# Attention, FFN and gate for one token: wide FFN reads, and the first and last DMA outside the block

## Chip, cores and metric

The kernel runs on one core of one Trainium2 chip. The metric is the device time of one execution in microseconds (us), of which the median of several runs is given. Engines are named as in the profile: PE does matmuls (PEld is its weight load), DVE is the vector engine, ACT the scalar engine, POOL GpSimd, SP the sync engine, which here only issues DMAs. A core has 16 DMA engines that all queues share.

## Reference

Four sequences (B = 4) decode one token each. Attention reads the last 4,096 positions of a cache with 8 key/value heads that 32 query heads share; beside it runs a gated FFN on the same `x`; a sigmoid gate mixes the two.

```python
x = A_x                                                   # 4 x 1 x 512, bf16
g = sigmoid((x * gate_w).sum(-1, keepdims=True))
# A: attention
q = (x @ wq) as 32 heads of 128
k, v = last 4096 positions of k_cache, v_cache            # 4 x 8 x 16384 x 128
p = softmax(q . k * 128 ** -0.5)
a = (p . v) as 4096 columns @ wo                          # wo: 4096 x 512
# B: FFN
gate = x @ W_gate;  up = x @ W_up                         # 512 x 1792 each
h = gate * (gate > 0) * up
b = h @ W_down                                            # 1792 x 512
return g * a + (1 - g) * b                                # 4 x 1 x 512
```

## The kernel before

The work on the caches is cut into NSET = 8 sets: set `s` is half of the key/value heads (four) of sequence `s // 2`. A set's keys are one load of 4 MB into `Ksb[:, s % 2]`, its values one of 4 MB into `Vsb[:, s % 2]`; each of the 128 partitions gets 32,768 contiguous bytes. So two sets of keys and two of values can be in SBUF or on their way, and a load waits until the set that used its buffer two before is done: the keys' load on the last scores (`SC`, s - 2), the values' load on the last `PV` of s - 2.

For each set, PE transposes the keys in place (L340, 16 groups of four, evicted by ACT at L345 or DVE at L347), computes scores (L373), DVE masks them and takes the maximum (L381, L388 to L402), ACT takes the exponent (L410), DVE transposes the probabilities (L417), PE multiplies with the values (L429), and `combine` sums the pieces and writes the set's normalised rows into `oq` (L450). The PE instructions of sets 2 to 7 run in a loop of three turns.

All large loads go through SP's DMA queue, in program order: `wq` (4 MB into `Wbig`, L245), K0, then K and V in turn, then behind V6 the two FFN matrices `W_gate` (L250) and `W_up` (L252), 1,792 KB each, into the free `Ksb[:, 0]`, then V7, then `W_down` (L255) into the free `Vsb[:, 0]`, then `wo` in four pieces (L260; 2,048, 1,280, 512 and 256 KB) into `Wbig`, where `wq` was. An FFN matrix of 1.8 MB lies in 128 partitions of 14,336 contiguous bytes: `(p t) f -> p (t f)` gives partition `p` four rows of `W_gate`, and `(p i) w -> p (i w)` fourteen rows of `W_down`. ACT's queue has two small loads, `x` (L243) and `gate_w` (L244).

At the end PE computes gate and up (`gateup`, L477), DVE makes `hT` (L481 to L483), PE does the last set's values and its `combine`, then `W_down` (L545) and `wo` (L553) into one PSUM bank `AB`. There the 512 output columns are cut into four blocks of 128: block `cb` accumulates in partitions 32 cb and on. `oq` and `hT` give each matmul 32 weight columns, of which columns 0, 8, 16 and 24 hold the four sequences and the rest are zero. So block `cb` of sequence `b` stands in row 32 cb + 8 b of `AB`. One DVE copy (L557) takes the bank to `outs`, 128 x 128, and the store (L558) reads every eighth row of it: 16 pieces of 256 bytes.

The program is first listed and then written out engine by engine (`Program`). An operation names the event that it gives and those that it waits for; `plan` works out the semaphore counts and leaves out waits already made; `put` writes the waits and the instruction; `emit` writes an engine's whole list. SP's list begins with the load of `wq` and ends with a bare wait for the store (L559). All five lists are written inside `nc.Block()` (L562): each engine branches into its part, and at the block's end all engines meet in a barrier, which the profile shows under L562. Ahead of the block stands another barrier, under L595, behind the setting of a few constants.

Of the kernel before, what the change touches and what calls it, by code (L numbers as in the profile page):

```python
# [6 lines left out]
BF16 = mybir.dt.bfloat16  # L7
ACTF = mybir.ActivationFunctionType
# [10 lines left out]
FF = 1792  # L19
NSET = 8  # L20
NFT = FF // 128
# [12 lines left out]
class Program:  # L34
# [69 lines left out]
            if name is not None:  # L104
                ins.then_inc(sems[self.events[name][0]], step)

    def emit(self, engine, eng, sems):
        ops, plan = self.ops[engine], self.plan(engine)
        if engine != "pe":
            for op, need in zip(ops, plan):  # L110
                self.put(eng, sems, op, need)
            return
        n = len(self.turns) - 1
        base = []
        for t in range(n + 1):
            level = {}
            for need in plan[:self.turns[t]]:
                level.update({s: v for s, v in need.items() if s in self.lowered})
            base.append(level)
        shift = [{s: base[t + 1].get(s, 0) - base[t].get(s, 0) for s in self.lowered} for t in range(n)]  # L120
        length = self.turns[1] - self.turns[0]
        bodies = []
        for t in range(n):
            assert shift[t] == shift[0] and self.turns[t + 1] - self.turns[t] == length
            body = []
            for k in range(length):
                need = plan[self.turns[t] + k]
                body.append({s: v - base[t].get(s, 0) for s, v in need.items() if s in self.lowered})
                if t > 0:
                    assert all(s in self.lowered for s in need), (t, k, need)  # L130
                    a, b = ops[self.turns[t] + k][1], ops[self.turns[0] + k][1]
                    assert (a is None) == (b is None) and (a is None or self.events[a][0] == self.events[b][0])
            bodies.append(body)
            assert body == bodies[0], [(k, x, y) for k, (x, y) in enumerate(zip(body, bodies[0])) if x != y]
        for k in range(self.turns[0]):
            self.put(eng, sems, ops[k], plan[k])
        for s, v in base[0].items():
            eng.sem_inc(sems[s], -v)
        with eng.Fori(0, n):
            for k in range(length):  # L140
                i = self.turns[0] + k
                need = dict(bodies[0][k])
                need.update({s: v for s, v in plan[i].items() if s not in self.lowered})
                self.put(eng, sems, ops[i], need)
            for s, v in shift[0].items():
                if v:
                    eng.sem_inc(sems[s], -v)
        for i in range(self.turns[n], len(ops)):
            self.put(eng, sems, ops[i], {s: v - base[n].get(s, 0) if s in self.lowered else v
                                         for s, v in plan[i].items()})  # L150


def bass_gated_mix__sliding_block_cached__glu_gated_reglu__decode_kernel(
# [13 lines left out]
    with ExitStack() as ctx:  # L167
        def sb(name, shape, dt):
            return ctx.enter_context(nc.sbuf_tensor(name, shape, dt))

        Ksb = sb("Ksb", [128, 2, 16384], BF16)
        Vsb = sb("Vsb", [128, 2, 16384], BF16)
# [30 lines left out]
        recip = sb("recip", [128, 2], FP32)  # L203
        oq = sb("oq", [128, 32, 32], BF16)
        gtmp = sb("gtmp", [128, NFT * 4], FP32)
        gtmp2 = sb("gtmp2", [128, NFT * 4], FP32)
        hT = sb("hT", [128, NFT, 32], BF16)
        outs = sb("outs", [128, 128], BF16)
        banks = [ctx.enter_context(nc.psum_tensor("bank%d" % i, [128, 512], FP32)) for i in range(8)]
        TR = banks[0:NTR]  # L210
        SCB = banks[NTR:NTR + NSC]
# [27 lines left out]
        def load_v(s):  # L239
            P.dma("sp", lambda e: e.dma_start(Vsb[:, s % 2, :], heads(A_v_cache, s)), ("V", s),  # L240
                  [("PV", s - 2, 3)] if s >= 2 else [], slot="v%d" % (s % 2))

        P.dma("act", lambda e: e.dma_start(xsb[0:4, :], A_x.rearrange("b o d -> (b o) d")), ("X",))  # L243
        P.dma("act", lambda e: e.dma_start(xsb[4:5, :], gate_w.rearrange("(o d) -> o d", o=1)), ("GW",))  # L244
        P.dma("sp", lambda e: e.dma_start(Wbig[:, :], A_wq.rearrange("(p t) w -> p (t w)", p=128)), ("WQ",))  # L245
        load_k(0)
        for s in range(1, NSET):
            load_k(s)
            load_v(s - 1)
        P.dma("sp", lambda e: e.dma_start(Ksb[:, 0, 0:4 * FF], B_W_gate.rearrange("(p t) f -> p (t f)", p=128)),  # L250
              ("WG",), [("SC", NSET - 2, NBANK - 1)])
        P.dma("sp", lambda e: e.dma_start(Ksb[:, 0, 4 * FF:8 * FF], B_W_up.rearrange("(p t) f -> p (t f)", p=128)),  # L252
              ("WU",), [("SC", NSET - 2, NBANK - 1)])
        load_v(NSET - 1)
        P.dma("sp", lambda e: e.dma_start(Vsb[:, 0, 0:NFT * 512], B_W_down.rearrange("(p i) w -> p (i w)", p=128)),  # L255
              ("WD",), [("PV", NSET - 2, 3)])
        wo_src = A_wo.rearrange("(p i) w -> p (i w)", p=128)
        for k in range(len(WO_CUTS) - 1):
# [178 lines left out]
        def combine(s):  # L437
            par, b, half = s % 2, s // 2, s % 2
            r = slice(64 * half, 64 * half + 64)
            for k in range(8):  # L440
                lo = 3 - k % 4 + 64 * (k // 4)
                P.op("pe", lambda e, k=k, lo=lo: e.matmul(FB[r, 256:288], Wsel[:, lo:lo + 64], osb[:, par, 32 * k:32 * k + 32],  # L442
                                                          start=(k == 0), stop=(k == 7)), None,
                     [("OSB", s), ("WSUM",), ("QC", 1), ("G",), ("OQ", s - 1) if s >= 1 else None, ("H",) if s == NSET - 1 else None])
            P.op("pe", lambda e: e.matmul(FB[r, 288:288 + NPIECE], Wsum[:, :], rowsum[:, par, :], start=True, stop=True),
                 ("SUMS", s))
            P.op("dve", lambda e: e.tensor_reduce(ssum[r, par:par + 1], FB[r, 288:288 + NPIECE], AXIS.X, ALU.add),
                 ("SSUM", s), [("SUMS", s)])
            P.op("dve", lambda e: e.reciprocal(recip[r, par:par + 1], ssum[r, par:par + 1]), ("RECIP", s), [("SSUM", s)])
            P.op("dve", lambda e: e.tensor_scalar(oq[r, :, 8 * b], FB[r, 256:288], recip[r, par:par + 1],  # L450
                                                  gsb[r, b:b + 1], op0=ALU.mult, op1=ALU.mult),
                 ("OQ", s), [("RECIP", s), ("G",), ("OQZ",)])

# [18 lines left out]
        def gateup():  # L472
            for i in range(NFT):
                for which, W, key in ((0, Wg, "WG"), (1, Wu, "WU")):
                    col = 64 + 64 * which + 4 * i
                    for t in range(4):
                        P.op("pe", lambda e, W=W, i=i, t=t, col=col: e.matmul(  # L477
                            FB[:, col:col + 4], W[:, t, i:i + NFT * 127 + 1:NFT], xT[:, t * 8:t * 8 + 4],
                            start=(t == 0), stop=(t == 3)),
                            ("GU",) if (i == NFT - 1 and which == 1 and t == 3) else None, [("WG",), ("WU",), ("OQ", NSET - 2)])  # L480
            P.op("dve", lambda e: e.tensor_scalar(gtmp[:, :], FB[:, 64:64 + NFT * 4], 0.0, None, op0=ALU.max), ("H0",), [("GU",)])  # L481
            P.op("dve", lambda e: e.tensor_tensor(gtmp2[:, :], FB[:, 128:128 + NFT * 4], gtmp[:, :], ALU.mult), ("H1",), [("H0",)])
            P.op("dve", lambda e: e.tensor_tensor(  # L483
                hT[:, :, :].rearrange("p i (b o) -> p i b o", o=8)[:, :, :, 0], gtmp2[:, :].rearrange("p (i b) -> p i b", b=4),
                gsb[:, 4:8].rearrange("p (o b) -> p o b", o=1).to_broadcast([128, NFT, 4]), ALU.mult), ("H",),
                [("H1",), ("G",), ("HZ",)])

# [61 lines left out]
        for k in range(len(WO_CUTS) - 1):  # L549
            for i in range(WO_CUTS[k], WO_CUTS[k + 1]):  # L550
                for cb in range(4):
# [2 lines left out]
                        AB[32 * cb:32 * cb + 32, 0:128], oq[:, i, :], Wo3[:, i, cb * 128:(cb + 1) * 128],  # L554
                        start=False, stop=(i == 31), tile_position=(0, 32 * cb)),
                        ("ACC",) if last else None, [("WO", k), ("OQ", NSET - 1)])
        P.op("dve", lambda e: e.tensor_copy(outs[:, :], AB[:, 0:128]), ("OUTS",), [("ACC",)])  # L557
        P.dma("sp", lambda e: e.dma_start(out.rearrange("b o (c d) -> c (b o) d", d=128), outs[0:128:8, :]), ("OUT",), [("OUTS",)])  # L558
        P.op("sp", None, None, [("OUT",)])  # L559

        sems = {name: ctx.enter_context(nc.semaphore(name)) for name in P.sems}
        with nc.Block() as block:  # L562
            @block.sync
            def _(e):
                P.emit("sp", e, sems)

            @block.gpsimd
            def _(e):
                P.emit("pool", e, sems)

            @block.tensor
            def _(e):
                P.emit("pe", e, sems)

            @block.vector
            def _(e):
                P.emit("dve", e, sems)

            @block.scalar
            def _(e):  # L580
                P.emit("act", e, sems)


# [26 lines left out]
```

## Time and profile before

| what | value |
|---|---|
| median of 3 runs | 197.55 us (197.55, 197.55, 197.69) |
| the profiled execution, its own time | 197.38 us |
| its span | 195.7 us |
| PE, DVE, ACT busy | 72%, 53%, 47% of the span |
| packets of SP's queue | 3,476, 81.01 MB |
| HBM read over the span | 414 GB/s |
| mean granted PE clock | 0.89 of full speed |
| first DMA of SP issued | 0.81 us |
| last matmul's result copied (L557) | 193.19 us |
| store issued (L558) | 193.51 us |

The span goes from the first to the last instruction that the profile shows; the execution's own time has in addition what lies before and after it. Times in the profile count from the span's start. A busy PE is not a PE at its peak, and idle time of an engine that isn't the bottleneck costs nothing. SP's issue of a DMA is not the transfer: between them stand the queue and what was queued before. The profile also keeps a record of each DMA packet (start, duration, bytes, queue), and among them the 4-byte writes by which each of the 16 engines reports the end of its share of a load; those are called landing records here.

### The profile page before, as it was taken

The numbers are of one execution on the slowest core, as the hardware profiler recorded it, in microseconds if no ns is written. First come the engines' busy times: TensorE is split into PE (matmuls) and PEld (weight loads), VectorE is DVE, ScalarE is ACT, GpSimd is POOL, SyncE is SP. The second block draws the span as 40 slices with busy tenths as digits, with TensorE's granted clock in tenths as the row PEclk, the third lists the DMA queues.
The fourth block names the chain that finished last, engine by engine and source line by source line (L and its number), as shares of the span: only waits on it lengthen the run. The fifth ranks groups of instructions, "written<-read, shape, count | busy, mean of one in ns | idle before, by whom it ended". The sixth has DMA issues, their size and how long they took to land.

```text
span 195.7 us, 4263 instructions
## 1 busy us (share of the span) xinstructions
PE 140.6 (72%) x1858; PEld 107.7 (55%) x1858; DVE 103.6 (53%) x278; ACT 91.5 (47%) x108; POOL 7.9 (4%) x39
## 2 busy tenths in 40 slices
PE   0134199968889919992999399929992999498634
PEld 0034197535567518751976286528752875397533
DVE  2102025888599456945585659456945584741200
ACT  2000058698398409760886098509750976220000
POOL 7400000000000000000000000000000000000000
PEclk9999999999999996997599879996996699965855
DMA  6999999999999999999999999999999999999991
GB/s 215 449 429 452 429 449 442 425 429 437 432 422 429 425 429 429 427 429 425 435 429 435 429 429 430 429 429 429 429 429 429 435 411 425 450 431 415 422 385 59
DMA packets 3498, 81.19 MB, mean 415 GB/s; under 512 B 409, under 2 KB 414, under 8 KB 670
## 3 DMA queue, kind: packets, MB, share of 16 engines
q1 hardware_dynamic: 3476, 81.01, 96.8%
q8 instruction: 9, 0.15, 0.3%
q14 instruction: 3, 0.02, 0.0%
q10 hardware_dynamic: 10, 0.01, 0.0%
HBM read 81.01 MB, written 0.00 MB: 414 GB/s over the span
## 4 chain that ended last, share of the span: by engine, by line
DMA 57%; PE 25%; ACT 9%; DVE 4%; issue 1%; SPq 1%
DMA Ksb<-in_A_k_cache_dram 46%; PE bank L340 16%; DMA Wbig<-in_A_wo_dram 12%; ACT Ksb L345 7%; PE bank L373 5%; DVE Ksb L347 2%; PE bank L429 2%; ACT sc L410 2%; PE bank L553 1%; PE bank L442 1%; DVE pT L417 1%; ACT L410 1%; DVE sc L381 1%; SPq L260 0%; DVE oq L450 0%
## 5 line engine op out<-in xcount | busy, mean ns | idle before, releaser
L345 ACT ACTIVATE Ksb<-bank 128x1024 bf16<-128x1024 bf16 x72 | 70.9, 1022 | 68.2 <-PE bank L340 68.0
L340 PE MATMUL bank<-identf,Ksb 128*128 128x128 f32 x512 | 81.1, 313 | 29.4 <-DMA Ksb<-in_A_k_cache_dram 24.0
L340 PEld LDWEIGHTS bank<-identf,Ksb 128*128 128x128 f32 x512 | 66.6, 161 | 44.1 <-DMA Ksb<-in_A_k_cache_dram 25.7
L347 DVE COPY Ksb<-bank 128x1024 bf16<-128x1024 bf16 x56 | 38.0, 685 | 41.8 <-PE bank L340 40.8
L381 DVE CUSTOM_DVE_ANT_0 sc<-bank,mask 128x512 bf16<-128x512 f32 x32 | 21.7, 684 | 9.6 <-PE bank L373 9.5
L429 PE MATMUL bank<-Vsb,pT 128*32 128x256 bf16 x512 | 20.8, 291 | 0.9 <-DMA Vsb<-in_A_v_cache_dram 0.9
L373 PE MATMUL bank<-Ksb,QSP 128*32 128x512 bf16 x256 | 19.4, 383 | 2.1 <-DVE Ksb L347 1.6
L410 ACT ACTIVATE sc<-sc,negmax 128x1024 bf16<-128x1024 bf16 x16 | 18.3, 1146 | 4.8 <-DVE negmax L402 4.7
L417 DVE STREAM_TRANSPOSE pT<-sc 128x1024 bf16<-128x1024 bf16 x16 | 19.7, 1237 | 1.3 <-ACT sc L410 1.0
L429 PEld LDWEIGHTS bank<-Vsb,pT 128*32 128x32 bf16 x512 | 13.2, 101 | 7.1 <-issue 3.3
L442 PEld LDWEIGHTS bank<-osb,Wsel 128*64 128x64 f32 x128 | 8.1, 138 | 4.6 <-issue 2.6
L442 PE MATMUL bank<-osb,Wsel 128*64 128x32 f32 x128 | 8.9, 224 | 1.2 <-DVE osb L434 1.2
L373 PEld LDWEIGHTS bank<-Ksb,QSP 128*32 128x32 bf16 x256 | 4.1, 94 | 9.4 <-DVE Ksb L347 4.4
L477 PE MATMUL bank<-xT,Ksb 128*128 128x4 bf16 x112 | 6.9, 199 | 1.8 <-DVE oq L450 1.8
L477 PEld LDWEIGHTS bank<-xT,Ksb 128*128 128x128 bf16 x112 | 6.8, 160 | 1.9 <-issue 1.9
L553 PE MATMUL bank<-Wbig,oq 128*32 128x128 bf16 x128 | 4.2, 311 | 4.1 <-DMA Wbig<-in_A_wo_dram 4.0
L357 POOL COPY QSP<-QS 128x64 bf16<-128x64 bf16 x8 | 1.8, 236 | 118.2 <-PE bank L373 107.4
L457 PE MATMUL bank<-xT,Wbig 128*128 128x4 bf16 x128 | 3.6, 166 | 4.0 <-DMA Wbig<-in_A_wq_dram 4.0
L306 PE MATMUL bank<-ident,xsb 5*128 5x5 bf16 x4 | 0.3, 167 | 7.9 <-DMA xsb<-in_gate_w_dram 7.9
L553 PEld LDWEIGHTS bank<-Wbig,oq 128*32 128x32 bf16 x128 | 3.1, 140 | 5.0 <-DMA Wbig<-in_A_wo_dram 5.0
L457 PEld LDWEIGHTS bank<-xT,Wbig 128*128 128x128 bf16 x128 | 3.5, 104 | 4.0 <-DMA Wbig<-in_A_wq_dram 4.0
L434 DVE COPY osb<-bank 128x256 f32<-128x256 f32 x8 | 3.4, 420 | 3.6 <-PE bank L429 3.6
(55 smaller groups left out, 47.0 us busy)
## 6 DMA issues: line engine op xcount, KB each, us to landing
Ksb<-in_A_k_cache_dram SPq DMA_DIRECT2D x8, 4096.0 KB, 22.9
Vsb<-in_A_v_cache_dram SPq DMA_DIRECT2D x8, 4096.0 KB, 32.0
Wbig<-in_A_wq_dram SPq DMA_DIRECT2D x1, 4096.0 KB, 12.2
Wbig<-in_A_wo_dram SPq DMA_DIRECT2D x1, 2048.0 KB, 20.2
Ksb<-in_B_W_gate_dram SPq DMA_DIRECT2D x1, 1792.0 KB, 17.9
Ksb<-in_B_W_up_dram SPq DMA_DIRECT2D x1, 1792.0 KB, 21.8
Vsb<-in_B_W_down_dram SPq DMA_DIRECT2D x1, 1792.0 KB, 15.6
Wbig<-in_A_wo_dram SPq DMA_DIRECT2D x1, 1280.0 KB, 22.8
```

The source lines that it names most:

```text
L340: P.op("pe", lambda e, bk=bk, cc=cc, c=c, s=s: e.transpose(bk[:, cc * 128:(cc + 1) * 128], kw[:, c * 128:(c + 1) * 128], identf[:, :]), (" ...
L345: P.op("act", lambda e: e.activation(dst, bk[:, :].bitcast(BF16), ACTF.Copy), ("KTC", s, i), [("KT", s, i)])
L347: P.op("dve", lambda e: e.tensor_copy(dst, bk[:, :].bitcast(BF16)), ("KTC", s, i), [("KT", s, i)])
L373: P.op("pe", lambda e, a=a, h=h: e.matmul(bk[32 * a:32 * a + 32, 0:512], QSP[:, s % 2, h, :], k4[:, 16 * bank:16 * bank + 16, 32 * a:32 * ...
L381: P.op("dve", lambda e: e.tensor_tensor_reduce(sc[:, s % 2, bank * 512:(bank + 1) * 512], bk[:, :], mask[:, :], 1.0, LOWEST, ALU.add, ALU.max,
L410: P.op("act", lambda e: e.activation(sc[:, par, k * PW:(k + 1) * PW], sc[:, par, k * PW:(k + 1) * PW], ACTF.Exp, bias=negmax[:, par:par + ...
L417: P.op("dve", lambda e: e.transpose(pT[:, par, k * PW:(k + 1) * PW], sc[:, par, k * PW:(k + 1) * PW]), ("PTT", s, k), [("EXP", s, k), ("PV ...
L429: P.op("pe", lambda e, c=c, g=g, col=col: e.matmul(OB[32 * g:32 * g + 32, 0:256], pT[:, par, col:col + 32], v3[:, 16 * k + c, :], start=(k ...
L442: P.op("pe", lambda e, k=k, lo=lo: e.matmul(FB[r, 256:288], Wsel[:, lo:lo + 64], osb[:, par, 32 * k:32 * k + 32], start=(k == 0), stop=(k ...
L457: P.op("pe", lambda e, h=h, t=t: e.matmul(FB[:, 64 + 4 * h:68 + 4 * h], Wq3[:, t, 128 * h:128 * h + 128], xT[:, t * 8:t * 8 + 4], start=(t ...
L477: P.op("pe", lambda e, W=W, i=i, t=t, col=col: e.matmul(FB[:, col:col + 4], W[:, t, i:i + NFT * 127 + 1:NFT], xT[:, t * 8:t * 8 + 4], star ...
L553: P.op("pe", lambda e, i=i, cb=cb: e.matmul(AB[32 * cb:32 * cb + 32, 0:128], oq[:, i, :], Wo3[:, i, cb * 128:(cb + 1) * 128], start=False, ...
```

## The change

1. `emit` takes a range of the engine's list. SP's first operation, the load of `wq`, is written before the block is entered; its last, the bare wait for the store, behind the block's end; all others inside as before.
2. A helper `wide` adds a DMA instruction whose two sides have different shapes. `W_gate`, `W_up` and `W_down` are read as 32 rows of 57,344 bytes; the destination stays 128 partitions of 14,336 bytes. Each row read fills four partitions. Bytes, order in the queue and waits are the same.
3. `oq` and `hT` hold the four sequences in the weight columns 0 to 3 in place of 0, 8, 16 and 24. Block `cb` of sequence `b` then stands in row 32 cb + b of `AB`.
4. `outs` is 4 x 512. Four copies bring the blocks there, 0 and 2 on DVE, 1 and 3 on ACT, and the store is 4 rows of 1,024 bytes, which waits for both engines.

```diff
-    def emit(self, engine, eng, sems):
+    def emit(self, engine, eng, sems, lo=0, hi=None):
         ops, plan = self.ops[engine], self.plan(engine)
         if engine != "pe":
-            for op, need in zip(ops, plan):
+            for op, need in list(zip(ops, plan))[lo:hi]:
                 self.put(eng, sems, op, need)
             return
...
-        outs = sb("outs", [128, 128], BF16)
+        outs = sb("outs", [4, 512], BF16)
...
+        def wide(e, dst, src):
+
+            return e.add_instruction(mybir.InstDMACopy(
+                mode="Copy", name=nc.get_next_instruction_name(), engine=e.engine, queue="qSPDynamicHW",
+                ins=[e.lower_ap_dma(src)[0]], outs=[e.lower_ap_dma(dst)[0]]))
...
-        P.dma("sp", lambda e: e.dma_start(Ksb[:, 0, 0:4 * FF], B_W_gate.rearrange("(p t) f -> p (t f)", p=128)),
+        P.dma("sp", lambda e: wide(e, Ksb[:, 0, 0:4 * FF], B_W_gate.rearrange("(p t) f -> p (t f)", p=32)),
               ("WG",), [("SC", NSET - 2, NBANK - 1)])
-        P.dma("sp", lambda e: e.dma_start(Ksb[:, 0, 4 * FF:8 * FF], B_W_up.rearrange("(p t) f -> p (t f)", p=128)),
+        P.dma("sp", lambda e: wide(e, Ksb[:, 0, 4 * FF:8 * FF], B_W_up.rearrange("(p t) f -> p (t f)", p=32)),
               ("WU",), [("SC", NSET - 2, NBANK - 1)])
         load_v(NSET - 1)
-        P.dma("sp", lambda e: e.dma_start(Vsb[:, 0, 0:NFT * 512], B_W_down.rearrange("(p i) w -> p (i w)", p=128)),
+        P.dma("sp", lambda e: wide(e, Vsb[:, 0, 0:NFT * 512], B_W_down.rearrange("(p i) w -> p (i w)", p=32)),
               ("WD",), [("PV", NSET - 2, 3)])
...
-            P.op("dve", lambda e: e.tensor_scalar(oq[r, :, 8 * b], FB[r, 256:288], recip[r, par:par + 1],
+            P.op("dve", lambda e: e.tensor_scalar(oq[r, :, b], FB[r, 256:288], recip[r, par:par + 1],
...
-                hT[:, :, :].rearrange("p i (b o) -> p i b o", o=8)[:, :, :, 0], gtmp2[:, :].rearrange("p (i b) -> p i b", b=4),
+                hT[:, :, 0:4], gtmp2[:, :].rearrange("p (i b) -> p i b", b=4),
...
-        P.op("dve", lambda e: e.tensor_copy(outs[:, :], AB[:, 0:128]), ("OUTS",), [("ACC",)])
-        P.dma("sp", lambda e: e.dma_start(out.rearrange("b o (c d) -> c (b o) d", d=128), outs[0:128:8, :]), ("OUT",), [("OUTS",)])
+        for c in range(4):
+            to, src = outs[0:4, 128 * c:128 * c + 128], AB[32 * c:32 * c + 4, 0:128]
+            if c % 2 == 0:
+                P.op("dve", lambda e, to=to, src=src: e.tensor_copy(to, src), ("OUTS", c), [("ACC",)])
+            else:
+                P.op("act", lambda e, to=to, src=src: e.activation(to, src, ACTF.Copy), ("OUTS", c), [("ACC",)])
+        P.dma("sp", lambda e: e.dma_start(out.rearrange("b o d -> (b o) d"), outs[:, :]), ("OUT",), [("OUTS", c) for c in range(4)])
         P.op("sp", None, None, [("OUT",)])
...
+        P.emit("sp", nc.sync, sems, 0, 1)
         with nc.Block() as block:
             @block.sync
             def _(e):
-                P.emit("sp", e, sems)
+                P.emit("sp", e, sems, 1, -1)
...
+        P.emit("sp", nc.sync, sems, -1)
```

## Prediction

> **What bounds the kernel now.** I read the views in this order: the page's 40 slices and its DMA queues, the chain of waits from its end backwards, the packet counts of two stretches, and the timeline of the first two and the last four microseconds. The median of the three runs is 197.55 us; the profiled execution took 197.38, of which its span is 195.66 (195.7 on the page) and 1.72 lies around it. The sum below is made against 197.38, and 0.17 is added at the end.
>
> The page, slices and queues (queue: packets, MB, share of 16 engines):
>
> ```profile
> DMA  6999999999999999999999999999999999999991
> ...
> q1 hardware_dynamic: 3476, 81.01, 96.8%
> q8 instruction: 9, 0.15, 0.3%
> ```
>
> Sixteen DMA engines are busy from the first slice to the last: the packet records have no idle moment on any of them between about 4 and 190 us. So what counts is when the slowest engine has moved its share of the 81 MB, and what lies before its first and after its last packet. Compute only waits. The end of the chain (start us, us, what):
>
> ```profile
> 168.06 22.77 DMA Wbig<-in_A_wo_dram
> 190.83 0.04 issue
> 190.87 1.85 PE bank L553 x56
> 192.72 0.01 issue
> 192.74 0.43 PE bank L553 x8
> 193.17 0.02 issue
> 193.19 0.29 DVE outs L557
> ```
>
> The last four loads are the pieces of `wo`, issued near 168 and landed behind everything queued before them. The packet records put the last byte of the last piece at 192.27; PE sees it at 192.73 and needs 0.43 for eight matmuls. PE also waited before pieces 1 and 2 (PEld 1.44 and 0.25 us), so a stream that ends earlier by a fraction of a microsecond takes the end with it.
>
> **The FFN reads.** 3 x 128 packets of 14,336 bytes become 3 x 32 rows of 57,344: each engine reads two rows for a matrix where it read eight, 18 packets fewer in all. The addresses and the partitions they fill are the same. What a packet costs beyond its bytes comes from two stretches of the queue, the first (129 to 157 us) with 32,768-byte packets alone, the second (160 to 166) with 14,336-byte ones:
>
> ```profile
> q1 hardware_dynamic: 411, 12.12, 100.6%
> ```
>
> ```profile
> q1 hardware_dynamic: 196, 2.58, 101.3%
> ```
>
> 12.12 MB are 370 data packets (the rest are 4-byte semaphore writes of 9 ns), so 1.006 x 16 x 28 us, less 0.37, over 370 gives 1.217 us a packet. 2.58 MB are 180 packets, so 1.013 x 16 x 6, less 0.14, over 180 gives 0.5395. The slope is 0.6775 us over 18,432 bytes, 36.76 ns a KB (of 1,000 bytes), and 0.5395 - 0.527 leaves 12.5 ns a packet. The landing records, 9.71 us for eight large packets and 4.30 for eight small ones, leave 10.8. 18 packets fewer are worth 0.19 to 0.23 us: I take **-0.21**. If that fixed part belongs to writing a partition's 14,336 bytes, which are as many as before, nothing is gained: 0 is the upper end inside this theory, and -0.25 the lower (the median packets, 1.214 and 0.539, leave 14 ns each).
>
> The Trainium skill speaks against this edit: DMA: Bandwidth & Descriptors, section Why small descriptors are slow, puts the fixed cost at about 3 cycles a packet and calls joining descriptors worth it only up to 256 bytes. With its 850 MHz, 18 x 3.5 ns would be 0.06, an estimate from that page, and the sum below would be 197.05 in place of 196.90. The trace's 11 to 12.5 ns are over three times as much, and I go by the trace.
>
> Where these loads land is covered: W_gate and W_up are down by 168.41 in the landing records, and PE reaches them at 170.89 behind `oq` of L450; W_down lands at 182.40 and is used from 183.97. If that cover were gone, a late row would stall PE by its lateness, but PE still has 2.87 us of waiting for the first piece of `wo`. SP issues them in 0.33 to 0.43 us, long before their turn.
>
> **The head.** The `wq` load leaves the block, still behind the launch barrier. Timeline of the first two microseconds:
>
> ```profile
> 0.80 0.56 ACTq L243 DMA_DIRECT2D xsb<-in_A_x_dram  x1
> ...
> 0.81 0.39 SPq L245 DMA_DIRECT2D Wbig<-in_A_wq_dram  x1
> ...
> 1.40 0.23 ACTq L244 DMA_DIRECT2D xsb<-in_gate_w_dram  x1
> ```
>
> SP leaves the barrier at 0.74 and issues at 0.81; only that step into the block is passed, no other SP instruction, and no other queue's. The first packet follows the issue by 1.02 us (1.83) and should move with it: **-0.05**, between -0.07 and 0.
>
> **The tail.** One 128x128 copy becomes four of 4x128, two on DVE and two on ACT; the store becomes four rows of 1,024 bytes instead of sixteen of 256; SP goes through the block's closing barrier first and waits for the store after it. What stands there now, timeline, then SP's waits, then the instructions of the block's line:
>
> ```profile
> 193.51 0.69 SPq L558 DMA_DIRECT2D out_dram<-outs  x1
> ```
>
> ```profile
> SPq L562 <- DMA out_dram<-outs: 1.1, 1, 1.1
> ```
>
> ```profile
> L562 SPq COMPARE_BRANCH  x1: 32/32/32, 195.3 to 195.3; - x1
> L562 SPq DRAIN  x1: 13/13/13, 195.4 to 195.4; - x1
> L562 SPq EVENT_SEMAPHORE  x1: 17/17/17, 195.6 to 195.6; - x1
> ```
>
> - Copies. A DVE copy of 128 columns took 0.29. Four small DVE operations on different partition groups are this row:
>
> ```profile
> 169.29 0.67 DVE L402 TENSOR_SCALAR negmax<-mall 32x1 f32<-32x1 f32 x4
> ```
>
> (0.67 - 0.145)/3 is 0.175 from start to start, 0.03 above one's 0.145; so a second copy adds up to 0.32, at least 0.15 if they overlap. ACT's pair is no later: 0.17 for the four columns of L318 and 0.83 ns a further column (1022 ns at 1024) make 0.28 each, and ACT has been idle since 172. **+0.28**.
> - SP now waits for two engines, ACT behind DVE: **+0.03** (0 to 0.06), a semaphore instruction of 17 ns and its neighbour. Behind this wait stands only the store.
> - The store. The old form had its first packet at 194.81, 1.30 after its issue began. The nearest row is the load of `x`, also four rows of 1,024 bytes: packet at 1.76 after an issue at 0.80, 0.96. **-0.34**; gate_w's single row (1.99 after 1.40) would make it -0.71, no change 0. From the last packet (194.93) to SP's release (195.28) stays 0.35.
> - The exit. From 195.28 to 195.66 SP branches, drains and passes the barrier, 0.38. In the new order this runs while the store is in flight (SP is free at about 194.3, the answer is due near 195.2), and 0.02 remains: **-0.36**, at worst 0 if the launch's end takes it back. Its cover is the store's 1.1 us; were that under 0.4, the rest would show again.
>
> Tail: 0.28 + 0.03 - 0.34 - 0.36 = -0.39. The new columns of `oq` and `hT` change strides, not shapes: 0 each, L450's 0.43 us being 3 us ahead of the first piece of `wo`.
>
> **Sum.** -0.21 - 0.05 - 0.39 = -0.65: 197.38 becomes 196.73, and against the median **196.90**.
>
> **Rivals.** *Half of it is empty*: the fixed cost sits on the writing side (0) and the store's latency does not depend on its form (0). Then -0.05 + 0.31 - 0.36 = -0.10, 197.45. For it: the page counts packets, not which side costs; against it: the same four-row form at the head answered in 0.96.
>
> *Long rows are slower.* Place: the three FFN loads. A single read of 57,344 bytes has to feed four partitions, and no row of this trace is longer than 32,768. The slowest packets here, the instruction fetches of 16,384 bytes, took 1.05 us, 15.6 bytes a ns. At that rate six rows an engine cost 22.0 us against 24 x 0.5395 = 12.9: +9.1, less 0.44 for the rest, 206.2. It decides already where a row takes over 2.29 us (25 bytes a ns; four packets now take 2.16), which makes the kernel slower by 0.2%. Against it: longer packets were always a little faster here, and the addresses stay in the same order.
>
> *A fetch strikes a late engine.* The engines end the first piece of `wo` between 185.21 and 187.30, though `wq` landed within 0.54 us on all: the landing records show each instruction fetch setting one engine back by about 1.5 us (at 177.83 one due at 180.51 landed at 182.05), and so far each struck an engine not struck before. Were an order of fetches changed so that one struck one of the last group, the end moves by +1.5: 198.4. For it: DVE, ACT and SP get other instruction counts; against it: PE, which has nearly all instructions, keeps its own.
>
> **How the numbers follow.** The likeliest as worked: 0.62, own range 196.4 to 197.2 (most of the store's bound on one side, of the exit's on the other). Half empty: 0.25. Long rows slow: 0.07. Fetch: 0.06. The range is **196.4 to 197.7**: it takes in the half-empty case and leaves the two slow ones, 0.13, and a little below. A measurement of this kernel tells about 0.2%, 0.4 us, from no change. Faster by more (under 197.15): 0.58 of the first case and 0.05 of the second, **0.63**; within: 0.04 and 0.19, **0.23**; slower: 0.13 and 0.01, **0.14**.
>
> **What would show it.** FFN packets of 57,344 bytes of about 2.11 us and a last `wo` byte near 192.0: right; 2.16, or packets still of 14,336: the first rival; over 2.29: the second. The store's first packet about 0.96 us after its issue, SP's closing barrier ahead of the store's landing, and a span that ends within 0.05 of SP's release. The `wq` issue near 0.76. A spread over 2.1 us between the first and the last engine's landing of `wo` speaks for the third. The prediction is wrong if any transfer starves a stage before 168 us, where I expect nothing to move by more than the head's 0.05.

## The result and the profile after

The changed kernel takes 196.70 us (median of 6 runs, 196.32 to 196.77) against 197.61 for the kernel before (median of 6, 197.50 to 198.00): ratio 0.9949, 95% interval 0.9936 to 0.9962, so 0.75 to 1.26 us less. The forecast was 196.9 in a range of 196.4 to 197.7, faster by 0.65. The profiled execution took 196.66 with a span of 195.33; what lies around the span is 1.33, where it was 1.72.

That last pair of numbers is the first thing to see. Between the two profiled executions the span lost 0.33 us, the remainder 0.39. The page after, slices and queues:

```profile
DMA  6999999999999999999999999999999999999892
...
q1 hardware_dynamic: 3176, 81.01, 97.0%
q8 instruction: 9, 0.15, 0.3%
```

300 packets fewer for the same 81.01 MB: the 384 FFN packets became 96, and 12 of the store's 16 are gone. The DMA engines are as full as before, and there are still nine instruction fetches. The end of the chain of waits (start us, us, what):

```profile
168.76 22.25 DMA Wbig<-in_A_wo_dram
191.05 1.84 PE bank L559 x44
```

The end still hangs on the last pieces of `wo`. In the packet records their last byte lands at 192.45, 0.18 later than before, although every byte is the same: the stream has not become shorter in this pair of executions. What got shorter lies behind it. Timeline of the last microseconds:

```profile
192.91 0.40 PE L559 MATMUL bank<-Wbig,oq 128*32 128x128 bf16 x8
193.37 0.56 ACT L568 ACTIVATE outs<-bank 4x128 bf16<-4x128 f32 x2 [20.60 <-PE bank L559]
193.37 0.59 DVE L566 CAST outs<-bank 4x128 bf16<-4x128 f32 x2 [7.43 <-PE bank L559]
194.03 0.35 SPq L569 DMA_DIRECT2D out_dram<-outs  x1
```

The instructions of the block's closing line (POOL's and SP's), and SP's waits (line; count; ns; first and last start):

```profile
L574 POOLq EVENT_SEMAPHORE  x2: 17/17/17, 194.6 to 194.7; - x2
...
L574 SPq DRAIN  x1: 167/167/167, 194.4 to 194.4; - x1
L574 SPq EVENT_SEMAPHORE  x1: 17/17/17, 194.7 to 194.7; - x1
```

```profile
L101 SPq EVENT_SEMAPHORE  x2: 17/17/17, 194.0 to 195.3; - x2
```

SP is through the barrier at 194.76 (POOL at 194.72), while the store is still on its way (its last packet ends at 194.97); SP's own wait, the second of L101, is released at 195.32 and is the span's last instruction. From the start of the first copy to the end of the span it was 195.66 - 193.19 = 2.47 before and is 195.33 - 193.37 = 1.96 now.

The stretch from 160 to 166 us of the FFN reads (packets, MB, share of 16 engines):

```profile
q1 hardware_dynamic: 57, 2.29, 89.6%
```

40 rows of 57,344 bytes; (0.896 x 16 x 6 - 0.15) / 40 is 2.147 us each. Four packets of before took 4 x 0.5395 = 2.158. Whether the stream gains this difference is asked under "What a packet costs beyond its bytes".

The head, timeline:

```profile
0.80 0.40 SPq L251 DMA_DIRECT2D Wbig<-in_A_wq_dram  x1
```

It is issued at 0.803 where it was 0.811, and the first packet starts at 1.83 as before.

### The profile page after: what moved, and what is told of

Read it like the earlier page. It is cut to its first block, busy times and chain, and to the rows that moved or that the text cites. A ratio compares the mean times of both kernels' runs of the same rounds, so it can differ in the third digit from the quotient of the medians.

```text
span 195.3 us, 4267 instructions
## 1 busy us (share of the span) xinstructions
PE 143.7 (74%) x1858; PEld 109.8 (56%) x1858; DVE 104.0 (53%) x279; ACT 92.2 (47%) x110; POOL 8.0 (4%) x39
## 3 DMA queue, kind: packets, MB, share of 16 engines
q1 hardware_dynamic: 3176, 81.01, 97.0%
HBM read 81.01 MB, written 0.00 MB: 415 GB/s over the span
## 4 chain that ended last, share of the span: by engine, by line
DMA 57%; PE 27%; ACT 8%; DVE 5%; issue 1%; SPq 1%; DVEq 0%
DMA Ksb<-in_A_k_cache_dram 45%; PE bank L346 18%; DMA Wbig<-in_A_wo_dram 11%; ACT Ksb L351 6%; PE bank L379 5%; DVE Ksb L353 3%; PE bank L435 2%; ACT sc L416 1%; PE bank L559 1%; PE bank L448 1%; DVE pT L423 1%; ACT L416 1%; DVE sc L387 1%; SPq L266 0%; SPq L245 0%
## 5 line engine op out<-in xcount | busy, mean ns | idle before, releaser
L346 PE MATMUL bank<-identf,Ksb 128*128 128x128 f32 x512 | 82.4, 316 | 28.2 <-DMA Ksb<-in_A_k_cache_dram 23.0
L448 PEld LDWEIGHTS bank<-osb,Wsel 128*64 128x64 f32 x128 | 8.8, 148 | 4.8 <-issue 2.8
L448 PE MATMUL bank<-osb,Wsel 128*64 128x32 f32 x128 | 9.7, 233 | 1.2 <-DVE osb L440 1.2
L568 ACT ACTIVATE outs<-bank 4x128 bf16<-4x128 f32 x2 | 0.5, 270 | 20.6 <-PE bank L559 20.6
```

Source lines behind the costliest of these rows:

```text
L346: P.op("pe", lambda e, bk=bk, cc=cc, c=c, s=s: e.transpose(bk[:, cc * 128:(cc + 1) * 128], kw[:, c * 128:(c + 1) * 128], identf[:, :]), (" ...
```

## Experiments

The ratio of each run is to the kernel before, measured on the same chip beside it; its median there was 197.61 in the first group, 197.55 in the second, 197.51 in the third. "Remainder" is a run's time less its span, as a median over its runs (spans are given to 0.1 us); for the kernel before it is 1.74 to 1.78.

**The theory after the result (T)**: nearly all of the gain is the place of SP's wait, half of it inside the span and half around it; the store's new form gives a little, long rows and head nothing. Against it: the prediction's own sizes (P), and that the remainder fell because of the store's form (S).

### One part at a time

Long rows alone (`e1_wide_only`):

```diff
-        P.dma("sp", lambda e: e.dma_start(Ksb[:, 0, 0:4 * FF], B_W_gate.rearrange("(p t) f -> p (t f)", p=128)),
+        P.dma("sp", lambda e: wide(e, Ksb[:, 0, 0:4 * FF], B_W_gate.rearrange("(p t) f -> p (t f)", p=32)),
...
```

> The kernel before with the three FFN matrices read in rows of 57,344 bytes and nothing else. Theory T (the gain sits in the place of the wait; a long row costs what its four parts did): FFN packets of 2.14 us, landings of each matrix 4.27 to 4.29 us apart, time lower by 0.00 to 0.06 us, ratio 0.9997 to 1.0. Theory P (the prediction: 12.5 ns less for each packet that falls away): packets of 2.11 us, time lower by 0.21, ratio 0.9989.

Measured: 197.53, ratio 0.9997 (0.9988 to 1.0006), remainder 1.73. Median packet 2.144 us, the landings of each of the two first matrices 4.29 us behind those of the load before it (mean of the 16 engines), as in the kernel before. The interval holds no change, and P's 0.9989 barely; packets and landings decide for T. By the landings nothing of the predicted gain is there.

The wait alone (`e2_exit_only`):

```diff
-                P.emit("sp", e, sems)
+                P.emit("sp", e, sems, 0, -1)
...
+        P.emit("sp", nc.sync, sems, -1)
```

> The kernel before with nothing changed but SP's wait for the store, which stands behind the block. Theory T: 0.36 us less inside the span and 0.39 less around it (1.72 to 1.33), so 0.75 in all, ratio 0.9962. Theory P: 0.36 inside the span and the same 1.72 around it, ratio 0.9982. Theory S (what lies around the span fell because of the store's new form): as P here.

Measured: 196.78, ratio 0.9958 (0.9945 to 0.9972), remainder 1.38. The block's line (POOL and SP) and SP's wait in this kernel:

```profile
L562 POOLq EVENT_SEMAPHORE  x2: 17/17/17, 194.9 to 194.9; - x2
...
L562 SPq DRAIN  x1: 423/423/423, 194.4 to 194.4; - x1
...
L562 SPq EVENT_SEMAPHORE  x1: 17/17/17, 195.0 to 195.0; - x1
```

```profile
L101 SPq EVENT_SEMAPHORE  x1: 17/17/17, 195.4 to 195.4; - x1
```

With the old store form the remainder fell all the same, so S is out, and P's 0.9982 lies outside the interval. This one edit carries 0.83 of the 0.91 us between the medians.

Copies, columns and store alone (`e3_store_only`), the wait inside the block:

```diff
-        P.op("dve", lambda e: e.tensor_copy(outs[:, :], AB[:, 0:128]), ("OUTS",), [("ACC",)])
+        for c in range(4):
+            to, src = outs[0:4, 128 * c:128 * c + 128], AB[32 * c:32 * c + 4, 0:128]
...
```

> The kernel before with columns 0 to 3, the four copies and the store of four rows; the wait stays inside the block. Theory T: from the end of the last matmul to the store's issue +0.33 us, from issue to first packet -0.53, so 0.20 less, ratio 0.9990, and 1.72 around the span. Theory P: +0.31 and -0.34, ratio 0.9998. Theory S: 0.20 less in the span and 0.39 less around it, ratio 0.9970.

Measured: 197.37, ratio 0.9987 (0.9978 to 0.9996), remainder 1.75. Timeline of its end:

```profile
193.45 0.56 ACT L562 ACTIVATE outs<-bank 4x128 bf16<-4x128 f32 x2 [21.55 <-PE bank L553]
193.45 0.59 DVE L560 CAST outs<-bank 4x128 bf16<-4x128 f32 x2 [8.39 <-PE bank L553]
194.10 0.35 SPq L563 DMA_DIRECT2D out_dram<-outs  x1
```

0.65 from copies to issue (0.32 before, so +0.33), and the packet records have the first packet at 194.88, 0.78 after the issue (1.30 before, so -0.52). By the rows that is 0.19 less, as T has it; P's 0.9998 is just outside the interval, and S is out again.

The changed kernel without the head (`e4_no_head`):

```diff
-        P.emit("sp", nc.sync, sems, 0, 1)
...
-                P.emit("sp", e, sems, 1, -1)
+                P.emit("sp", e, sems, 0, -1)
```

> The changed kernel with the load of wq back inside the block, all else as changed. Theory T: SP's first issue 0.01 us later, time as the changed kernel's within 0.05, ratio to the kernel before 0.995. Theory P: 0.05 later, ratio 0.9952.

Measured: 196.63, ratio 0.9947 (0.9933 to 0.9960), remainder 1.29. Inside or outside the block, the load of `wq` is issued at 0.803: the head is worth nothing that can be seen.

### Where the 0.4 us around the span went

Theory E: after the barrier each engine has a way out of the program that the profile does not show. Before, all five began it together at the span's end; now four begin it 0.6 us earlier and only SP's own still follows the store. Rival B: it matters only that no barrier stands behind the store. All five engines wait (`e5_all_wait`):

```diff
-        P.emit("sp", nc.sync, sems, -1)
+        nc.sync.wait_ge(sems["d_OUT"], 16)
+        nc.gpsimd.wait_ge(sems["d_OUT"], 16)
+        nc.tensor.wait_ge(sems["d_OUT"], 16)
+        nc.vector.wait_ge(sems["d_OUT"], 16)
+        nc.scalar.wait_ge(sems["d_OUT"], 16)
```

> The changed kernel, but all five engines wait for the store behind the block, not SP alone. Theory E (the 0.39 us less around the span is the other engines' way out of the program, which runs while SP alone still waits): span as changed, 195.3 to 195.5, but around it 1.7 to 1.8 again, time 0.3 to 0.5 above the changed kernel's 196.7, ratio 0.997. Theory B (it is the barrier that no longer stands behind the store): around it 1.3 as changed, ratio 0.995.

Measured: 197.14, ratio 0.9982 (0.9973 to 0.9990), remainder 1.77, span as in the changed kernel. No barrier stands behind the store here, and yet the remainder is back. B is out.

The same edit with one engine in place of SP:

> The changed kernel, but ACT in place of SP waits for the store behind the block. Theory E: ACT's own way out decides; if all engines' ways are alike, 196.7 as with SP; if they differ, up to 0.4 more or less than that. Theory B: 196.7.

> The changed kernel, but POOL in place of SP waits for the store behind the block. Theory E: 196.7 if the ways out are alike, up to 0.4 more or less if not. Theory B: 196.7.

> The changed kernel, but PE in place of SP waits for the store behind the block. Theory E: 196.7 if the ways out are alike, up to 0.4 more or less if not. Theory B: 196.7.

> The changed kernel, but DVE in place of SP waits for the store behind the block. Theory E' (each engine has its own way out; the span's remainder was 1.31 us with SP waiting, 1.43 with ACT, 1.53 with PE, 1.77 with POOL): a remainder between 1.3 and 1.8, time 196.6 to 197.2. If the remainder is 1.3 or less whichever engine but POOL waits, the table of the others is chance.

| who waits for the store | median us | ratio (interval) | remainder us |
|---|---|---|---|
| in the block, before the barrier | 197.61, 197.55, 197.51 | 1 | 1.74 to 1.78 |
| SP (the changed kernel) | 196.70 | 0.9949 (0.9936 to 0.9962) | 1.31 |
| DVE | 196.64 | 0.9954 (0.9940 to 0.9967) | 1.34 |
| ACT | 196.68 | 0.9959 (0.9946 to 0.9972) | 1.43 |
| PE | 196.88 | 0.9966 (0.9954 to 0.9979) | 1.53 |
| POOL | 197.16 | 0.9984 (0.9975 to 0.9992) | 1.77 |
| all five | 197.14 | 0.9982 (0.9973 to 0.9990) | 1.77 |

The last instruction of the span with POOL waiting, from the line of that wait:

```profile
L595 POOLq EVENT_SEMAPHORE  x1: 17/17/17, 195.2 to 195.2; - x1
```

In that execution the span is 0.16 shorter than the changed kernel's, 195.18, and the run still takes longer: POOL's way out is some 0.45 us longer than SP's and sets the end whenever POOL waits, alone or with the others. (A remainder also holds what lies before the span; only the differences between engines are read here.) That fits E, and it explains the kernel before: there POOL left the barrier within 0.1 us of all the others, and the remainder is POOL's, 1.74 to 1.78. With SP waiting, POOL leaves at 194.72, so 194.72 + 1.77 = 196.49 against SP's 195.33 + 1.31 = 196.64: SP's end is the later one by only 0.15. In the run with the wait alone the barrier is later, and the two are level: POOL 194.96 + 1.77 = 196.73, SP 195.44 + 1.31 = 196.75. The step from SP to DVE and ACT is within the spread of the runs.

What a way out consists of stays open, since the profile does not show it. A closing handshake that passes the engines in a fixed order would give such a table as well as five separate ways of different length, and no run here tells the two apart.

### A store in two halves

If a store's answer goes with its rows, two stores of eight rows on two queues would beat both kernels (`e10_two_stores`; the wait behind the block, one copy, old columns):

```diff
+        for h, q in ((0, "sp"), (1, "act")):
+            P.dma(q, lambda e, h=h: e.dma_start(out.rearrange("b o (c d) -> c (b o) d", d=128)[2 * h:2 * h + 2],
+                                                outs[64 * h:64 * h + 64:8, :]), ("OUT", h), [("OUTS",)])
+        P.op("sp", None, None, [("OUT", 0), ("OUT", 1)])
```

> The kernel before with the wait behind the block, one 128x128 copy, columns 0, 8, 16, 24, and two stores of eight rows of 256 bytes, blocks 0 and 1 by SP, 2 and 3 by ACT; SP waits for both. Against the run with the wait alone behind the block (196.8): if a store's time to its first packet goes with its rows ([4,4] took 1.30 us, [4,1] 0.77), about 1.0 us, and 0.2 to 0.3 less, 196.5, ratio 0.9945, faster than the changed kernel; if it goes with the number of its dimensions, 1.3 as before and 196.8, ratio 0.996.

Measured: 196.96, ratio 0.9970 (0.9958 to 0.9982): a miss. Timeline:

```profile
193.59 0.67 SPq L559 DMA_DIRECT2D out_dram<-outs  x1
193.59 0.64 ACTq L559 DMA_DIRECT2D out_dram<-outs  x1
```

Each half takes nearly as long to issue as the whole did (0.69), and its first packet is 1.27 us behind its issue on SP and 1.53 on ACT. Going from 16 rows to 8 changed little. The forms with a faster answer have their rows one behind the other in one dimension, but also fewer and longer ones (at most four, of 1,024 bytes); no run has few rows in two dimensions, so which of the two makes them fast is not shown. Part of the miss lies elsewhere: SP's drain at the block's end takes 696 ns here, against 423 with one store of this form, POOL leaves the barrier only at 195.14, and its 195.14 + 1.77 = 196.91 is as late as SP's 195.56 + 1.31 = 196.87.

### What a packet costs beyond its bytes

By the packets' durations the long rows gained 0.011 us for three packets saved, 4 ns each, where the prediction had 12.5. Is the rest a cost of the piece written? First only the writes are cut (`e11_dest_cut`: the two matrices' tiles get a pitch of 1,808 elements, the reads stay 14,336 bytes), then both (`e12_both_cut`):

```diff
-        Wg = Ksb[:, 0, 0:4 * FF].rearrange("p (t f) -> p t f", t=4)
+        Wg = Ksb[:, 0, 0:4 * (FF + 16)].rearrange("p (t f) -> p t f", t=4)[:, :, 0:FF]
...
```

> The kernel before with W_gate and W_up written into four pieces of 3,584 bytes a partition, 32 bytes apart; the reads stay rows of 14,336 bytes. Theory W (the 11 to 12.5 ns that a packet costs beyond its bytes belong to the piece written): 24 pieces more an engine and matrix, each landing 0.26 to 0.30 us later, packets of about 0.575, time up by 0.5 to 0.6, ratio 1.0028. Theory R (they belong to the row read): packets of 0.539, time as before, ratio 1.0.

> The kernel before with W_gate and W_up read in rows of 3,584 bytes and written into pieces of 3,584, 32 bytes apart. Theory W: little beyond the run that cuts the writes alone (the long rows gained 3 ns a packet, so up to 24 x 3 ns a matrix, 0.14 us in all). Theory R: 24 rows more an engine and matrix, +0.5 to +0.6 us in all, where the run with only the writes cut shows none of it.

Measured: 197.86, ratio 1.0014 (1.0005 to 1.0023), and 197.97, ratio 1.0021 (1.0011 to 1.0031). The same stretch from 160 to 166 us, writes cut, then both cut:

```profile
q1 hardware_dynamic: 191, 2.51, 102.7%
```

```profile
q1 hardware_dynamic: 700, 2.45, 102.5%
```

175 rows of 14,336 bytes: (1.027 x 96 - 0.14) / 175 = 0.5626 us, 0.0231 above the uncut 0.5395, so 7.7 ns for each of three more pieces written. 684 rows of 3,584: (1.025 x 96 - 0.14) / 684 = 0.1437, four make 0.5746, 0.0120 above, so 4 ns for each of three more rows read.

But the records of neighbouring packets overlap, which the shares above 100% hint at. In the kernel before, eight packets of 0.5395 make 4.316 us, and the landings of two loads are only 4.292 apart; in the run with both cut, 32 of 0.1437 make 4.597, and the landings are 4.479 apart. So a record's duration is not what the stream pays for the packet; the landing records tell that. From the landing of V6, the load ahead of the two matrices, to that of `W_up`, as a mean over the 16 engines:

| reads and writes of the two matrices | us |
|---|---|
| rows of 14,336, pieces of 14,336 (the kernel before and three runs) | 8.584 to 8.587 |
| rows of 57,344, pieces of 14,336 (the changed kernel and seven runs) | 8.582 to 8.583 |
| rows of 14,336, pieces of 3,584 (writes cut) | 8.941 |
| rows of 3,584, pieces of 3,584 (both cut) | 8.958 |

48 more pieces written an engine cost 0.355 us, 7.4 ns each; 48 more rows read cost 0.017, 0.35 ns each; 12 rows fewer gained 0.001 to 0.005, at most 0.4 ns each. So the cost sits with the piece written, as W says, and R is out. The size that W gave it, 11 to 12.5 ns, was too large: 0.355 by the landings and 0.35 between the medians, where it had 0.5 to 0.6. Two things stay open. The pieces cost 8.6 ns each in `W_gate` and 6.2 in `W_up`, which start at different places in the partition, so their place may count beside their number. And by its landings a packet of 14,336 bytes costs about 9.5 ns beyond its bytes (4.292 us for eight against 9.71 for eight of 32,768), 2 more than the 7.4.

The Trainium skill (DMA: Bandwidth & Descriptors, Why small descriptors are slow) puts about 3 cycles on a packet, 3.5 ns at its 850 MHz, an estimate from that page. In this case neither side comes to that by the landings: 0.4 ns or less for a row read, 7.4 for a piece written.

## Why the prediction was right, term by term

The range and the direction held. The sum of 0.65 was 0.26 short of the medians' 0.91, and its terms were less good than it:

| step of the prediction | predicted us | measured us |
|---|---|---|
| FFN in long rows | -0.21 | -0.01 to 0.00 by the landings |
| head | -0.05 | 0.00 (issued at 0.803 with the head and without it) |
| copies and the second wait | +0.31 | +0.33 |
| the store's answer | -0.34 | -0.52 |
| the store's packets, first to last | 0 | +0.04 (0.12 before, 0.17 after) |
| exit, inside the span | -0.36 | -0.36 (0.38 before, 0.02 left) |
| exit, around the span | 0 | -0.39 |
| sum | -0.65 | -0.90 to -0.91; between the medians -0.91 |

**The FFN rows.** The mechanism was named with its alternative: "If that fixed part belongs to writing a partition's 14,336 bytes, which are as many as before, nothing is gained". That is what the runs showed: -0.21 became nothing, because 7.4 ns belong to the piece written and at most 0.4 to the row read. The error is a choice: two packet sizes that differ on both sides at once can't say which side a cost belongs to, and I took the end that the whole cost gave.

**The head.** The row was read too closely: 0.07 us between barrier and issue looked like the step into the block, but outside the block SP needs 0.06 as well, and the changed kernel without the head issues at 0.803 too.

**The store.** The nearest row by form, the load of `x`, gave 0.96 to the first packet, and it was 0.78. That load is the first DMA on ACT's queue and took 0.56 to issue; the store, a later one on SP's, took 0.35. Whether the place in the queue, the queue or the direction makes the difference is not shown.

**The exit.** Inside the span it is exact. Around it the working had "at worst 0 if the launch's end takes it back" and no bound on the other side. The remainder, 1.72 us, was treated as a constant. It is not: it depends on which engine leaves last (1.31 to 1.77), and the change lets four engines leave early. That the sum came as near as it did is partly luck: 0.26 that it counted for FFN rows and head was not there, and 0.57 that it did not count, 0.18 at the store and 0.39 around the span, was.

**The rivals.** "Half of it is empty" was right about the writing side, wrong about the store. Long rows are not slower (their landings come at the same distance). There were nine fetches as before, and the last engine of the first `wo` piece landed at 187.47, against 187.30.

No version beats the changed kernel beyond the intervals: without its head (196.63), or with DVE waiting (196.64), it is the same, and the wait's move alone (196.78) is within 0.1 of it.

## What to carry to other kernels

The wait for the last store is best put behind everything that all engines do together, on an engine whose own way out is short, and never on the one that has the longest way: here moving the wait was worth some 0.75 to 0.83 us, about four times what the store's form gave, and the longer reads gave nothing. Treat the time around the span as work with a critical engine of its own, to be bounded like any other term. Before a larger DMA row is credited with saved packets, separate what is paid for a row read from what is paid for a piece written, and take both from the distance between landings, since the records of neighbouring packets overlap.

## What the runs showed of the hardware that was not expected

- The ways out of the program differ by engine: with SP or DVE leaving last the remainder is 1.31 and 1.34 us, with POOL 1.77.
- Beyond its bytes a row read costs 0.4 ns or less (rows of 3,584 to 57,344 bytes) and a piece written 7.4 ns (3,584 against 14,336), by the landings. The packets' own durations said 4 and 7.7: their records overlap.
- The first packet of a store of [4 rows] of 1,024 bytes comes 0.78 us after its issue begins, of [4,4] pieces of 256 bytes 1.30, of eight such pieces 1.27 on SP and 1.53 on ACT beside it. The Trainium skill (DMA: Bandwidth & Descriptors, Latency and other measured facts) has about 0.6 us to the first byte on these queues; only the single row of `gate_w`, 0.59, comes to that here.
- SP's drain at the block's end is 13 ns behind a landed store, but 167 ns behind the issue of the one-dimensional store, 423 behind the [4,4] one and 696 in the run with two. In the changed kernel the store's flight hides it; in the run with two stores the late barrier makes POOL's end as late as SP's.
- The stream's last byte is no constant of the bytes: 192.27 in the profiled execution before, 192.45 after, 192.88 in the run without the head, where the first `wo` piece landed on the 16 engines between 185.16 and 187.91. One profiled pair can't tell 0.2 us of a stream's length; the mean distance between landings told 0.005.
